# Layer 2's output columns parted as 256 and 320 instead of 288 and 288

## The chip, the cores and the metric

The kernel runs on one core of a Trainium2 chip. A core has a matrix engine (TensorE, "PE" in the profile, with its weight loads shown apart as "PEld"), a vector engine (VectorE, "DVE"), an activation engine (ScalarE, "ACT"), a general one (GpSimd, "POOL") and one that only issues transfers (SyncE, "SP"). The engines run at the same time and wait for each other by semaphores. [...] The metric is the device time of one execution in microseconds, the median of three runs for the kernel before.

## The reference

Two blocks work on 2048 tokens of 576 features, and their results are joined:

```
xn = layernorm(x)                                   # x: 2048 x 576
s  = S4D(xn)                                        # long convolution by FFT over the 2048 tokens
y  = layernorm(xn)
h  = gelu(y @ w1 + b1)                              # w1: 576 x 4608
g  = silu(h @ w2 + b2)                              # w2: 4608 x 576
out = x + s * g
```

The change is in the product `h @ w2`, called layer 2 below. Everything is float32 outside; the two large products are made from a rounded high part and a low rest, so that three fast products (high by high, high by low, low by high) give one accurate one.

## The kernel before

The MLP walks over 48 slots. The tokens come in two halves, each half in two blocks `tb` of 512 tokens; the 4608 hidden features come in 12 groups `g` of 3 x 128. A slot is one group for one block. It has 11 positions: three of layer 1 and eight of layer 2.

Layer 1 (`layer1`, line 529) makes 128 hidden features for 512 tokens with 14 matmuls, whose moving side is 512 columns wide. ScalarE then applies the gelu (line 547) and rounds the high part `hh` (line 550), and VectorE makes the low part `hl` (line 553).

Layer 2 (`layer2`, line 556) takes the 128 tokens `j` (0 to 3) of the block as stationary side and rows of w2 as moving side. w2's tiles are `w2h` (high) and `w2l` (low), each 128 partitions of 3 rows of 576 float32, 2304 bytes a row. [...] Each part of a block of 128 tokens takes three rows `i` by three products, nine matmuls (line 568). In a slot that makes 4 x 2 x 9 = 72, in the kernel 3456, half of them for each part. The result tile `q` has two banks: part 0 begins at the start of the first bank and part 1 at the start of the second. Tiles `mxa` and `mxb` take turns. When both parts are done, VectorE adds all 576 columns to the running sum `acc` in one instruction (line 576).

Only for the last 128 tokens of the last slot is each part added as soon as it is there (`halves`, line 1435); `finish` (line 633) then makes that part's silu (line 642), two VectorE steps (lines 647 and 657) and its output transfers (line 660). For the first half of the tokens, `gate_store` (line 584) makes a tanh over the two halves of 288 columns of the finished sum; the change leaves it alone.

The order of the work is written out ahead of time by a planner (`Order`, line 52). Steps have an engine, an estimated duration and a due time; the planner fills each engine's line between the matmuls, and the instructions of every engine are pinned in that order. Layer 2's estimated lengths stand in a list (line 1177), the additions' in line 1440. Beside the MLP run the pieces of the convolution (names `cv`, `kt`, `A2`, `f2t`, `g2t`), whose matmuls are put in between positions. Weights come in through the SP queue, which the change does not touch.

Of the kernel before, what the change touches and what calls it, by code (L numbers as in the profile page):

```python
# [17 lines left out]
L, D, N, F = 2048, 576, 128, 4608  # L18
# [14 lines left out]
G = 3  # L33
NG = F // (P * G)
KB = 4
TB = 512

def dve(n):  # L40
    return 0.075 + 0.00104 * n


def act(n):
    return 0.06 + 0.00098 * n
# [159 lines left out]
def step(eng, dur, fn, need=(), mark=None, cv=0, at=0.0, late=0.0, tbl=None, by=1e9):  # L205
    return dict(eng=eng, dur=dur, fn=fn, need=tuple(need), mark=mark, cv=cv, at=at, late=late, tbl=tbl, by=by)
# [3 lines left out]
def mixer_kernel(ctx, tc, u, log_a_real, a_imag, c_real, c_imag, log_dt, d_skip, w1, b1, w2, b2,  # L210
                 f1, f2, g2, g1, tvals, ident, out, parts=("mlp", "s4d")):
    nc = tc.nc
# [6 lines left out]
    def bank2(name):  # L219
        return ps.tile([P, 2, TB], F32, name=name, bufs=2 if name == "cv" else 1)  # L220

# [29 lines left out]
    bias2 = sb.tile([P, D], F32, name="bias2")  # L251
# [102 lines left out]
    acc = sb.tile([P, 8, D], F32, name="acc")  # L354
# [71 lines left out]

    XH = sb.tile([P, KB, 2, TB], F32R, name="XH")
    XL = sb.tile([P, KB, 2, TB], F32R, name="XL")
    XR = sb.tile([P, 2, TB], F32R, name="XR")
    dsk = sb.tile([P, D // 4], F32, name="dsk")  # L430
# [92 lines left out]
    HID, LAST, Q1, Q2 = {}, {}, {}, {}  # L523
    turn = [0]

    def mx(i):
        return "mxa" if (turn[0] + i) % 2 == 0 else "mxb"

    def layer1(g, tb, i):
# [11 lines left out]
        if i == 0:  # L541
            HID[tb] = (sb.tile([P, G, TB], F32R, name="hh"), sb.tile([P, G, TB], F32R, name="hl"))
        hh, hl = HID[tb]
        t = sb.tile([P, TB], F32, name="h32", bufs=2)

# [10 lines left out]
    def layer2(g, tb, j, terms, last):  # L556


        h, lo = W[2]
        hh, hl = HID[tb]  # L560
        c = slice(j * P, (j + 1) * P)
        if j not in Q2:
            Q2[j] = bank2(mx(j + 1))
        q = Q2[j]
        for i, dh in terms:
            d = slice(dh * 288, dh * 288 + 288)
            for k, (a, b) in enumerate(((hh, h), (hh, lo), (hl, h))):
                nc.tensor.matmul(q[:, dh, :288], a[:, i, c], b[:, i, d], start=i == 0 and k == 0,  # L568
                                 stop=i == G - 1 and k == 2)
        if last:  # L570
            Q2.pop(j)

        def add(dh, n):
            o = acc[:, tb * 4 + j].rearrange("p (h d) -> p h d", h=2)[:, dh:dh + n]
            b = bias2.rearrange("p (h d) -> p h d", h=2)[:, dh:dh + n]
            nc.vector.tensor_add(o, q[:, dh:dh + n, :288], b if g == 0 else o)  # L576
        return add

    def tanh_half(z):
# [19 lines left out]
    def rows_at(t, b, c0, c1):  # L599
        return [dram(t, (b + 16 * y) * D + c0, [[32 * D, 64], [1, c1 - c0]]) for y in range(2)]  # L600
# [32 lines left out]
    def finish(b, c0, c1, silu, end):  # L633

        c = slice(c0, c1)
        z = acc[:, b - 8, c]
        n = c1 - c0
        T = []

        def act_z():  # L640
            T.append(sb.tile([P, D], F32, name="row", bufs=NROW)[:, c])
            nc.scalar.activation(T[0], z, AF.Silu if silu else AF.Tanh, scale=1.0 if silu else 0.5)

        def mul():
            s = XS[b][1][:, c]
            if silu:
                nc.vector.scalar_tensor_tensor(s, s, 2.0, T[0], op0=OP.mult, op1=OP.mult)
            else:
                nc.vector.tensor_mul(s, s, z)

        def mul2():
            s = XS[b][1][:, c]
            nc.vector.scalar_tensor_tensor(s, T[0], 1.0, s, op0=OP.add, op1=OP.mult)

        def total():
            x, s = XS[b]
            nc.vector.tensor_add(x[:, c], x[:, c], s[:, c])
            for y, o in enumerate(rows_at(out, b, c.start, c.stop)):
                queue = nc.scalar if end and y else nc.sync
                queue.dma_start(o, x[64 * y:64 * y + 64, c])  # L660
        st = [step("ACT", act(n), act_z, tbl="silu" if silu else "gelu"), step("DVE", dve(n), mul)]
        if not silu:
            st.append(step("DVE", dve(n), mul2))
        return st + [step("DVE", dve(n), total)]
# [444 lines left out]
    NSLOT = 4 * NG  # L1109
# [142 lines left out]
    def wmark(n, which):  # L1252

        per = KB + 1 + G
        a = n * per + (0 if which == 1 else KB + 1)
        return [("w", k) for k in range(a, a + (KB + 1 if which == 1 else G))]
# [123 lines left out]
    def hidden_by(pos, i, o=0):  # L1380
        n = when(pos, o + (G if i < G - 1 else G + 2))
        low = n - dve(TB) - GAP
        high = low - act(TB) - GAP
        free = when(pos, o + (2, G, G + 1)[i])
        return min(high, free) - act(TB) - GAP, high, low
# [4 lines left out]
    def look_ahead(pos):  # L1390
        a, d = [], []
        for q in range(pos + 1, pos + 1 + NPOS):
            o, r = q // NPOS * NPOS, q % NPOS
            if r < G:
                b = hidden_by(pos, r, o)
                a.append(b[0])
                d.append(b[2])
            elif r - G in (2, 3, 5, 7):
                d.append(add_by(pos, (2, 3, 5, 7).index(r - G), o))
        od.next = dict(ACT=min(a), DVE=min(d))  # L1400

    for slot in range(NSLOT):
        turn[0] = slot
        g, tb = slot // 2 % NG, slot % 2
        n = slot // 2
        final = slot >= NSLOT - 2
        for pos in range(NPOS):
            if pos < G:
                need = wmark(n, 1) + [("x", tb)]
                if pos == 0:  # L1410
                    od.force(lambda: all(m in od.marks for m in need))
                cell = []
                od.unit(lambda: cell.append(layer1(g, tb, pos)), L1, need)
                look_ahead(pos)
                a, b, c = cell[0]
                by = hidden_by(pos, pos)
                od.urgent.append((od.t["PE"], [step("ACT", 0.62, a, tbl="gelu", by=by[0]),
                                               step("ACT", act(TB), b, by=by[1]),
                                               step("DVE", dve(TB), c, mark=("h", slot, pos), by=by[2])]))
                od.advance(od.t["PE"])  # L1420
                if pos == G - 1 and tb == 1 and slot + 1 < NSLOT:
                    weigh_in(1)
            else:
                j, terms, last, hid = l2_terms(pos - G)
                need = wmark(n, 2) + [("h", slot, i) for i in hid]
                if pos == G:

                    pe_turns()
                od.force(lambda: all(m in od.marks for m in need))
                if max(od.marks[m] for m in need) > od.t["PE"] + 0.3:  # L1430
                    pe_turns(any_time=True)
                cell = []
                od.unit(lambda: cell.append(layer2(g, tb, j, terms, last)), LEN[pos], need)
                look_ahead(pos)
                halves = slot == NSLOT - 1 and j == 3
                if last or halves:
                    add = cell[0]
                    dh, k = (terms[0][1], 1) if halves else (0, 2)
                    done = ("acc", slot, j, dh)
                    chain = [step("DVE", dve(288 * k), lambda: add(dh, k), mark=done, by=add_by(pos, j))]  # L1440
                    if final:
                        b = 8 + 4 * tb + j
                        x = el if slot < NSLOT - 1 else od.line()
                        st = finish(b, dh * 288, (dh + k) * 288, slot == NSLOT - 1, halves)
                        st[0]["need"] = (done, ("s8", b - 8))
                        x["steps"] += st
                    elif g == NG - 1:
                        for d in range(2):
                            one, two = gate_store(4 * tb + j, d)
                            by = od.t["PE"] + 5.0  # L1450
                            chain += [step("ACT", act(288), one, tbl="gelu", by=by), step("DVE", dve(288), two, by=by)]
                    od.urgent.append((od.t["PE"], chain))
                if pos == NPOS - 1 and tb == 1 and slot + 1 < NSLOT:
                    weigh_in(2)
            for f in LATER.get((slot, pos), ()):
                f()
            od.advance(od.t["PE"])
            pe_turns(all_lines=pos in (0, 1, 2, G + 1, G + 3, G + 5, NPOS - 1))
# [55 lines left out]
```

## Time and profile before

| What | Value |
|---|---|
| Median of 3 runs (lowest to highest) | 1124.04 us (1123.22 to 1124.32) |
| Profiled execution: its time, its span | 1126.06 us, 1124.3 us |
| PE busy, share of the span | 1106.2 us, 98% |
| Weight loads | 957.3 us, 85% |
| DVE busy | 880.0 us, 78% |
| ACT busy | 666.0 us, 59% |
| Mean granted clock of PE | 0.994 |
| Instructions | 26828 |

A matmul's duration in the profile reaches from its start to the end of its drain, and the next one starts before that; so the groups' mean durations are longer than the distance between two starts, and a long row of matmuls counts as one busy stretch. Weight loads run beside the matmuls. In the groups, `128*128 128x288` means a stationary side of 128 by 128 and a moving side of 128 partitions by 288 columns. Rows of the order of time give start and duration in microseconds; "x4" joins four of one kind. "Idle before" is the idle time of that engine ahead of an instruction, with what ended it.

### The profile page before, as it was taken

What the parts mean: (1) busy time and instruction counts of PE and PEld (TensorE: products, weight loads), DVE (VectorE), ACT (ScalarE), POOL (GpSimd) and SP (SyncE); (2) the same over time, 40 slices, a digit from 0 to 9 for tenths busy, and PEclk for the clock granted to TensorE, in tenths of its full rate; (3) what the DMA queues carried; (4) which work ended last, traced back from release to release, by engine and by line L of the source; (5) the groups of instructions that cost most, each with busy time, mean ns of one, the idle gap of its engine ahead of it and who ended that gap; (6) DMA issues with size and microseconds to landing.
All of it is one profiled execution on the core that took longest, in us unless ns stands there. A gap on an engine that the chain in (4) does not pass through costs nothing.

```text
span 1124.3 us, 26828 instructions
## 1 busy us (share of the span) xinstructions
PE 1106.2 (98%) x11355; PEld 957.3 (85%) x11355; DVE 880.0 (78%) x1475; ACT 666.0 (59%) x1011; POOL 183.1 (16%) x253
## 2 busy tenths in 40 slices
PE   9799999999999999999999999999999999999997
PEld 7698988988888788888888888887888978888896
DVE  6487688698879787999899889986898876555356
ACT  5297399976566475677956755654657433342233
POOL 5546401135110100001100010000000021112300
PEclk9899999999999999999999999999999999999999
DMA  7544645535353420443424242332315154534513
GB/s 217 208 152 122 219 159 183 162 113 126 106 167 92 107 82 13 142 108 104 155 56 137 34 123 56 111 85 63 91 50 126 33 169 136 163 103 142 151 60 85
DMA packets 111048, 132.39 MB, mean 118 GB/s; under 512 B 59660, under 2 KB 78192, under 8 KB 110352
## 3 DMA queue, kind: packets, MB, share of 16 engines
q1 hardware_dynamic: 96144, 79.88, 25.9%
q0 software_dynamic: 14304, 50.05, 14.1%
q8 instruction: 89, 1.46, 0.6%
q10 hardware_dynamic: 480, 0.74, 0.3%
q14 instruction: 31, 0.25, 0.1%
HBM read 101.87 MB, written 36.63 MB: 123 GB/s over the span
## 4 chain that ended last, share of the span: by engine, by line
PE 94%; issue 2%; DMA 1%; DVE 1%; ACT 1%; SPq 0%; POOL 0%; POOLq 0%; DVEq 0%; ACTq 0%
PE mxb L540 20%; PE mxb L568 20%; PE mxa L540 20%; PE mxa L568 20%; PE cv L885 3%; PE cv L1013 3%; PE cv L1055 2%; PE cv L986 2%; PE cv L955 2%; PE cv L1081 2%; DMA tv<-in_tvals_dram 1%; DMA kt<-in_A_A_imag_dram 1%; DMA raw<-in_B_w_dram 0%; PE cv L448 0%; DVE acc L576 0%
## 5 line engine op out<-in xcount | busy, mean ns | idle before, releaser
L553 DVE TENSOR_TENSOR hl<-h,hh 128x512 fp32r<-128x512 f32 x144 | 99.3, 692 | 129.4 <-ACT hh L550 128.9
L568 PE MATMUL mxb<-w2h,hh 128*128 128x288 f32 x576 | 172.2, 299 | 0.7 <-DVE acc L576 0.7
L568 PE MATMUL mxa<-w2h,hh 128*128 128x288 f32 x576 | 171.0, 297 | 0.0
L568 PE MATMUL mxb<-w2h,hl 128*128 128x288 f32 x576 | 170.3, 296 | 0.0
L568 PE MATMUL mxa<-w2h,hl 128*128 128x288 f32 x576 | 170.1, 295 | 0.0
L568 PE MATMUL mxb<-w2l,hh 128*128 128x288 f32 x576 | 169.4, 294 | 0.0
L568 PE MATMUL mxa<-w2l,hh 128*128 128x288 f32 x576 | 169.4, 294 | 0.0
L547 ACT ACTIVATE h<-mxb,b1t 128x512 f32<-128x512 f32 x72 | 49.6, 689 | 157.1 <-PE mxb L540 154.9
L568 PEld LDWEIGHTS mxb<-w2h,hh 128*128 128x128 f32 x576 | 108.1, 188 | 9.3 <-issue 4.1
L568 PEld LDWEIGHTS mxa<-w2h,hh 128*128 128x128 f32 x576 | 108.1, 188 | 6.2 <-issue 1.4
L568 PEld LDWEIGHTS mxa<-w2l,hh 128*128 128x128 f32 x576 | 108.2, 188 | 0.8
L568 PEld LDWEIGHTS mxb<-w2l,hh 128*128 128x128 f32 x576 | 108.2, 188 | 0.5
L568 PEld LDWEIGHTS mxb<-w2h,hl 128*128 128x128 f32 x576 | 108.1, 188 | 0.2 <-DVE hl L553 0.2
L568 PEld LDWEIGHTS mxa<-w2h,hl 128*128 128x128 f32 x576 | 108.1, 188 | 0.0
L786 POOL DMA_DIRECT2D par<-par_s x36 | 27.3, 760 | 479.6 <-DVE mg L829 475.5
L547 ACT ACTIVATE h<-mxa,b1t 128x512 f32<-128x512 f32 x72 | 49.6, 689 | 85.3 <-PE mxa L540 84.8
L576 DVE TENSOR_TENSOR acc<-mxb,acc 128x576 f32<-128x576 f32 (+1 forms) x89 | 66.3, 745 | 36.1 <-PE mxb L568 35.9
L550 ACT ACTIVATE hh<-h 128x512 fp32r<-128x512 f32 x144 | 90.6, 630 | 3.7
L576 DVE TENSOR_TENSOR acc<-mxa,acc 128x576 f32<-128x576 f32 x88 | 66.2, 752 | 28.3 <-PE mxa L568 27.6
L540 PE MATMUL mxa<-XH,w1h 128*128 128x512 f32 x288 | 81.7, 404 | 0.4 <-ACT XH L452 0.4
L540 PE MATMUL mxb<-XH,w1h 128*128 128x512 f32 x288 | 80.2, 401 | 0.1
L540 PE MATMUL mxb<-XL,w1h 128*128 128x512 f32 x288 | 78.1, 393 | 0.0
(215 smaller groups left out, 2395.2 us busy)
## 6 DMA issues: line engine op xcount, KB each, us to landing
raw<-in_B_w_dram SPq DMA_DIRECT2D x72, 288.0 KB, 3.2
raw<-in_B_w_dram SPq DMA_DIRECT2D x96, 192.0 KB, 3.6
par_s<-A POOLq DMA_DIRECT2D x4, 2160.0 KB, 8.1
par<-par_s POOLq DMA_DIRECT2D x36, 240.0 KB, 3.3
f2t<-f2q SPq DMA_DIRECT2D x24, 256.0 KB, 3.7
g2t<-g2p SPq DMA_DIRECT2D x24, 256.0 KB, 3.9
raw<-in_B_w_dram SPq DMA_DIRECT2D x48, 96.0 KB, 4.3
xc<-xn_s SPq DMA_DIRECT2D x48, 96.0 KB, 3.8
```

The costliest lines, as they stand in the source:

```text
L540: nc.tensor.matmul(q, a, b, start=j == 0, stop=j == len(ops) - 1)
L547: nc.scalar.activation(t, q, AF.Gelu_apprx_tanh, bias=b1t[:, g * G + i:g * G + i + 1], scale=1.0)
L550: LAST[0] = nc.scalar.activation(hh[:, i], t, AF.Copy)
L553: nc.vector.tensor_sub(hl[:, i], t, hh[:, i].bitcast(F32))
L568: nc.tensor.matmul(q[:, dh, :288], a[:, i, c], b[:, i, d], start=i == 0 and k == 0, stop=i == G - 1 and k == 2)
L576: nc.vector.tensor_add(o, q[:, dh:dh + n, :288], b if g == 0 else o)
L786: nc.gpsimd.dma_start(PAR[b].rearrange("p (g i) k -> p g (i k)", g=4), dram(par_s, (b // 3 * 48 + b % 3 * 4) * NPAR, [[D * NPAR, P], [12 * ...
L885: nc.tensor.matmul(q[32 * g:32 * g + 32, i // 2, i % 2 * 64:i % 2 * 64 + 64], U[:, ri, 4 * g + i, :], v[:, ri, 4 * g + i, :], start=ri == ...
L955: nc.tensor.matmul(Q[24 * v][:, e].rearrange("p d b -> p b d"), f1t[r, 0].rearrange("p f k -> p (f k)"), XC[i][r, :, 12 * e:12 * e + 12], ...
L986: nc.tensor.matmul(Q[g // 2 * 2][:, g % 2], f1t[r, (e + g) % 2].rearrange("p f k -> p (f k)"), KT[c, i][r, :, 32 * e:32 * e + 32], start=e ...
L1013: nc.tensor.matmul(Q[i][32 * q:32 * q + 32, f, 2 * ri:2 * ri + 2], m[r, 4 * i + q, 32 * ri:32 * ri + 32], A2[r, 4 * p + 2 * i + q // 2, :, ...
L1055: nc.tensor.matmul(QI[q // 2][64 * f:64 * f + 64, q % 2, i], MAT["g2t", p + i // 2][r, i % 2, f, ri], YS[p + i // 2][0][r, i % 2, ri, f], ...
```

## The change

Part 0 takes columns 0 to 255 and part 1 columns 256 to 575, so that the parts begin at bytes 0 and 1024 of a row of w2 (before: 0 and 1152). In PSUM the two parts now lie side by side across the border of the two banks: part 0 fills the last 256 places of the first bank, part 1 the first 320 of the second. The addition reads one run of 576 values instead of two runs of 288 with a gap. For the last 128 tokens the parts that are finished one by one have 256 and 320 columns. The planner's list of layer 2's lengths and the additions' estimate stay as they are.

```diff
 TB = 512
+DH = (0, 256, D)
...
         if j not in Q2:
-            Q2[j] = bank2(mx(j + 1))
+            Q2[j] = bank2(mx(j + 1)).rearrange("p h n -> p (h n)")
         q = Q2[j]
         for i, dh in terms:
-            d = slice(dh * 288, dh * 288 + 288)
+            d = slice(DH[dh], DH[dh + 1])
             for k, (a, b) in enumerate(((hh, h), (hh, lo), (hl, h))):
-                nc.tensor.matmul(q[:, dh, :288], a[:, i, c], b[:, i, d], start=i == 0 and k == 0,
-                                 stop=i == G - 1 and k == 2)
+                nc.tensor.matmul(q[:, TB - DH[1] + d.start:TB - DH[1] + d.stop], a[:, i, c], b[:, i, d],
+                                 start=i == 0 and k == 0, stop=i == G - 1 and k == 2)
...
         def add(dh, n):
-            o = acc[:, tb * 4 + j].rearrange("p (h d) -> p h d", h=2)[:, dh:dh + n]
-            b = bias2.rearrange("p (h d) -> p h d", h=2)[:, dh:dh + n]
-            nc.vector.tensor_add(o, q[:, dh:dh + n, :288], b if g == 0 else o)
+            d = slice(DH[dh], DH[dh + n])
+            o = acc[:, tb * 4 + j, d]
+            nc.vector.tensor_add(o, q[:, TB - DH[1] + d.start:TB - DH[1] + d.stop], bias2[:, d] if g == 0 else o)
         return add
...
-                        st = finish(b, dh * 288, (dh + k) * 288, slot == NSLOT - 1, halves)
+                        st = finish(b, DH[dh], DH[dh + k], slot == NSLOT - 1, halves)
```

## The prediction

> **What bounds the kernel now.** I read the page from the top (busy shares, then the chain that ended last), then the busy time by stretch, then the groups of matmuls by shape, and last the order of time in the last two slots. The page's head, its clock row and its chain:
>
> ```profile
> span 1124.3 us, 26828 instructions
> ...
> PE 1106.2 (98%) x11355; PEld 957.3 (85%) x11355; DVE 880.0 (78%) x1475; ACT 666.0 (59%) x1011; POOL 183.1 (16%) x253
> ...
> PEclk9899999999999999999999999999999999999999
> ...
> PE 94%; issue 2%; DMA 1%; DVE 1%; ACT 1%; SPq 0%; POOL 0%; POOLq 0%; DVEq 0%; ACTq 0%
> ```
>
> Two stretches of the table of busy time, one from the middle and the last (columns: stretch, its length, then busy time of PE, weight loads, DVE, ACT and POOL, granted clock, DMA share, GB/s):
>
> ```profile
> 300.00:400.00 100.00, 100.00 (x1216) 85.26 (x1215) 81.56 (x137) 60.24 (x83) 9.46 (x14) 1.00 0.43 118
> 1100.00:1124.00 24.00, 16.32 (x101) 14.74 (x99) 14.34 (x23) 8.77 (x13) 0.00 (x0) 0.92 0.37 87
> ```
>
> TensorE makes 94% of the chain. In the middle it is busy for 100.00 of 100.00 us at clock 1.00, while DVE is busy for 81.56. So the time is the number of matmuls times the distance between the starts of two of them, and then a tail. The change touches the matmuls of line 568, so their form and the forms next to it matter:
>
> ```profile
> L568 PE MATMUL mxb<-w2h,hh 128*128 128x288 f32 x576 | 172.2, 299 | 0.7 <-DVE acc L576 0.7
> L540 PE MATMUL mxb<-XL,w1h 128*128 128x512 f32 x288 | 78.1, 393 | 0.0
> L1013 PE MATMUL cv<-A,f2t 64*32 64x192 f32 x1536 | 38.6, 333 | 0.0
> L986 PE MATMUL cv<-kt,f1t 32*128 32x384 f32 x192 | 18.9, 507 | 0.0
> L568 PEld LDWEIGHTS mxb<-w2h,hh 128*128 128x128 f32 x576 | 108.1, 188 | 9.3 <-issue 4.1 <-DVE acc L576 1.5 <-ACT hh L550 0.9
> L1081 PEld LDWEIGHTS cv<-A,g1t 128*64 128x64 f32 x96 | 6.4, 134 | 7.9 <-issue 7.5
> L885 PEld LDWEIGHTS cv<-v,U 128*32 128x32 f32 x2304 | 33.8, 110 | 9.4 <-issue 9.1 <-DVE hl L553 0.4
> ```
>
> Line 568 stands in six such groups of 576, so 3456 matmuls: 1728 for the left half of the columns, 1728 for the right. The 299 ns of one is from its start to the end of its drain; the next starts before that, so the cost is the distance of starts. That is read in order of time. Here are the first matmuls of four runs of nine in the last slot but one (left, right, left, right half; rows between left out), then the first of layer 1, and another 14 matmuls later:
>
> ```profile
> 1092.06 0.30 PE L568 MATMUL mxb<-w2h,hh 128*128 128x288 f32 x1
> ...
> 1093.25 0.29 PE L568 MATMUL mxb<-w2h,hh 128*128 128x288 f32 x1
> ...
> 1094.45 0.29 PE L568 MATMUL mxa<-w2h,hh 128*128 128x288 f32 x1
> ...
> 1095.63 0.29 PE L568 MATMUL mxa<-w2h,hh 128*128 128x288 f32 x1
> ...
> 1096.83 1.08 PE L540 MATMUL mxb<-XH,w1h 128*128 128x512 f32 x4
> ...
> 1100.02 1.07 PE L540 MATMUL mxa<-XH,w1h 128*128 128x512 f32 x4
> ```
>
> The 36 matmuls of 288 columns take 1096.83 - 1092.06 = 4.77 us, 132.5 ns each. The 14 of 512 columns take 3.19 us, 227.9 ns each. That is (227.9 - 132.5) / 224 = 0.426 ns for a column, and 132.5 - 288 x 0.426 = 9.8 ns for a matmul whatever its width.
>
> **The change part by part.**
>
> *Columns.* Each left matmul loses 32 columns and each right one gains 32: 132.5 - 13.6 = 118.9 ns and 132.5 + 13.6 = 146.1 ns. The pair stays at 265.0 ns, the count stays at 3456, and so do the weight loads. Sum over 1728 pairs: 0.
>
> *The start of the right part.* It moves from byte 1152 of a row of w2's tiles to byte 1024. The four runs above show what a start at 1152 costs now: left (start 0) 1.19 and 1.18 us, right 1.20 and 1.20 us, so 2.37 / 18 = 131.7 ns against 2.40 / 18 = 133.3 ns. Rows are cut to 10 ns, so the gap of 1.6 ns has about a nanosecond of doubt. Taken over the start times of all the matmuls of line 568 whose successor is of that line (distances under 160 ns), the means are 131.6 ns left and 133.0 ns right, a gap of 1.4 ns. The first and the last of them:
>
> ```profile
> L568 PE MATMUL mxb<-w2h,hh x576: 288/294/402, 24.1 to 1116.5; 128*128 128x288 f32 x192
> ...
> L568 PE MATMUL mxb<-w2h,hl x576: 289/295/398, 24.4 to 1116.7; 128*128 128x288 f32 x192
> ```
>
> If that gap is the price of the start, 1.4 x 1728 = 2.4 us are to be had. Upwards, the new widths could carry the gap with them and double it, +2.4 us. Downwards, if both parts fell by one and a half times the gap, 2.1 x 3456 = 7.3 us. I take 0, because right and left differ in their PSUM bank and in their place in the order too, so that the rows don't tie the gap to the start. [...]
>
> *The weight load under a narrower matmul.* Each matmul has its own load of 128 columns, issued when the matmul before it starts. In the last slot TensorE once waited for a result to be read, and there the load shows uncovered:
>
> ```profile
> 1114.56 0.29 PE L568 MATMUL mxb<-w2h,hl 128*128 128x288 f32 x1
> 1115.05 0.45 DVE L576 TENSOR_TENSOR acc<-mxb,acc 128x288 f32<-128x288 f32 x1
> ...
> 1115.56 0.19 PEld L568 LDWEIGHTS mxb<-w2h,hh 128*128 128x128 f32 x1 [0.93 <-DVE acc L576]
> 1115.56 0.40 PE L568 MATMUL mxb<-w2h,hh 128*128 128x288 f32 x1 [0.70 <-DVE acc L576]
> 1115.66 0.19 PEld L568 LDWEIGHTS mxb<-w2l,hh 128*128 128x128 f32 x1
> 1115.79 0.29 PE L568 MATMUL mxb<-w2l,hh 128*128 128x288 f32 x1
> ```
>
> The next start is 0.23 us later instead of 0.13, so the load itself takes 0.10 us. The groups of loads say the same: 110, 134 and 188 ns for 32, 64 and 128 columns, (188 - 110) / 96 = 0.81 ns for a column, 104 ns for 128, and some 84 ns of latency that overlaps. Transposes, whose moving side is 128 wide and which each have a load of 128 columns, start every 0.11 us ((0.60 - 0.27) / 3):
>
> ```profile
> 10.96 0.60 PE L448 MATMUL cv<-idp,row 128*128 128x128 f32 x4
> 11.29 0.14 PEld L448 LDWEIGHTS mxb<-idp,row 128*128 128x128 f32 x1
> 11.39 0.27 PE L448 MATMUL mxb<-idp,row 128*128 128x128 f32 x1
> ```
>
> So 104 to 110 ns of load have to fit under 118.9 ns: covered, with 9 to 15 ns to spare instead of 23 to 29. From below it costs 0. From above, the 256 columns could cost no less than 288 do now: 13.6 x 1728 = 23.5 us. I take 0, by the load that stands uncovered in this very group.
>
> *DVE's addition (line 576).* Its PSUM input becomes one run of 576 instead of two of 288, the same number of elements; its price now:
>
> ```profile
> L576 DVE TENSOR_TENSOR acc<-mxa,acc 128x576 f32<-128x576 f32 x88 | 66.2, 752 | 28.3 <-PE mxa L568 27.6
> L576 DVE TENSOR_TENSOR acc<-mxb,acc 128x288 f32<-128x288 f32 x2 | 0.9, 454 | 0.9 <-PE mxb L568 0.9
> ```
>
> It is taken as 752 ns again. TensorE covers it: the group of line 568 above waits for DVE 0.7 us in the whole run. If each of the 192 additions were 10% longer and uncovered, 14 us; but the 28.3 us of idling ahead of 88 of them is 0.32 us each, cover for the 0.08.
>
> *Planner.* The costs that the order of work is planned with stay as they were (288 a half) save in the last block's closing steps, so instructions, queues and DMAs keep their order and count.
>
> *Tail.* Only the last block works half by half. Its closing rows now:
>
> ```profile
> 1116.73 0.29 PE L568 MATMUL mxb<-w2h,hl 128*128 128x288 f32 x1
> 1117.05 0.46 DVE L576 TENSOR_TENSOR acc<-mxb,acc 128x288 f32<-128x288 f32 x1 [0.89 <-PE mxb L568]
> 1117.43 0.75 DVE L647 SCALAR_TENSOR_TENSOR A<-A,row 128x576 f32<-128x576 f32 x1
> 1118.21 0.76 DVE L657 TENSOR_TENSOR v<-v,A 128x576 f32<-128x576 f32 x1
> 1118.89 0.45 DVE L647 SCALAR_TENSOR_TENSOR A<-A,row 128x288 f32<-128x288 f32 x1
> 1119.37 0.46 DVE L657 TENSOR_TENSOR v<-v,A 128x288 f32<-128x288 f32 x1
> 1119.75 0.45 DVE L647 SCALAR_TENSOR_TENSOR A<-A,row 128x288 f32<-128x288 f32 x1
> 1120.23 0.46 DVE L657 TENSOR_TENSOR v<-v,A 128x288 f32<-128x288 f32 x1
> ```
>
> A column costs DVE (752 - 454) / 288 = 1.03 ns, so 32 columns are 0.03 us. The left addition (1115.05) starts when DVE is free, not when TensorE is, so its earlier input gives nothing; it is 0.03 shorter. The nine right matmuls then take 9 x 13.6 = 0.12 us longer and the right addition 0.03 longer; the two steps left and two right that follow cancel. Sum: +0.12 us. The wait of 0.7 us could go, since the halves lie in separate banks; it is there now although they do already, so I leave it: at best -0.9 us. The last output rows are 1280 bytes instead of 1152, at most 0.1 us more.
>
> **Sum.** 0 + 0 + 0 + 0.12 = +0.1 us. The profiled execution took 1126.06 us, its span 1124.3 and 1.8 around it; it would go to 1126.2. The median of the runs is 1124.04 (1123.22 to 1124.32), 2.0 lower, so the forecast is 1124.2 us. A difference under 0.2% (2.2 us) counts as none: it is about what a measurement of this kernel can tell from no change.
>
> **The rivals.**
>
> *Slower: the load no longer fits.* Place: the 1728 left matmuls. If a matmul can begin only when both the stream before it and its load are done, and the hand-over of 9.8 ns comes after the later of the two, the distance is 104 to 110 plus 9.8 and 3 for the load's later start, 117 to 123 ns against 118.9. At 123 it is 4.1 x 1728 = +7.1 us, 1131 us; it decides (over 2.2 us) from 120.2 ns on. For it: the loads' busy share of 85%, and no row with such a narrow matmul of this type and load. Against it: the transposes' 0.11. [...]
>
> *Faster: the start was the gap.* The right matmuls then run with the left ones' fixed part: -2.4 us, with the tail 1121.8 us; more, if the left gains too, down to 1117. For it: the gap is there in every pair of runs. Against it: bank and order differ as well.
>
> *Far slower: the fast rate ends at 256 columns.* Lines 1013 and 986 run the full type, (507 - 333) / 192 = 0.91 ns a column, against (393 - 299) / 224 = 0.42 for 568 and 540. At that rate 256 columns cost 0.49 x 256 = 125 ns more, 1728 times: +216 us, 1340 us. No row is narrower than 288 in the fast type, so the trace can't exclude it.
>
> **How the numbers follow.** No change 0.34; the load 0.30; the start 0.28; the rate 0.05; a slower tail or DVE in the way 0.03. So faster 0.28, same 0.34, slower 0.38. The likeliest alone: 1122 to 1126.4. Since the other two hold more than half, the range takes them in: down to 1117 (both parts gaining) and up to 1136 (the load at 125.7 ns). That leaves out the rate and the ends of the others, under 0.2.
>
> **What would show it.** The distance of starts in line 568: 118.9 and 146.1 ns, sum 265.0. If the load is in the way, the left ones stand at 120 to 126 and the right ones at 146; if the start matters, the right ones stand below 145; if the rate ends, the left ones stand near 240. DVE's 752 ns and the one wait of 0.7 us stay. Wrong would be a pair off 265.0 by more than 1.3 ns, or new idle time ahead of line 568.

## The result and the profile after

The changed kernel took 1126.65 us (median of 9 runs, 1125.95 to 1128.37); the kernel before took 1124.40 us beside it (9 runs, 1122.40 to 1125.18). The ratio is 1.0024, with a 95% interval of 1.0014 to 1.0035: slower by a quarter of a per cent. The forecast was 1124.2 us in a range of 1117 to 1136, with no change (within 0.2%) as the likeliest case. The time lies in the range, 0.25 us above the band of the likeliest case (1122 to 1126.4); the interval of 0.14 to 0.35% doesn't shut out a difference under 0.2%.

The page of the changed kernel, the lines that answer to those shown of before (line numbers are higher by one):

```profile
span 1124.7 us, 26828 instructions
...
PE 1107.8 (98%) x11355; PEld 958.8 (85%) x11355; DVE 880.1 (78%) x1475; ACT 666.0 (59%) x1011; POOL 183.1 (16%) x253
...
PE 96%; DVE 1%; DMA 1%; ACT 1%; SPq 0%; issue 0%; ACTq 0%
```

The instructions are the same in number on every engine, and TensorE still makes the chain. So the cause has to be sought in the distances between matmuls. The same four runs of nine as in the prediction (left, right, left, right part, then layer 1), in the order of time of TensorE:

```profile
1092.30 0.28 PE L569 MATMUL mxb<-w2h,hh 128*128 128x256 f32 x1
...
1093.38 0.31 PE L569 MATMUL mxb<-w2h,hh 128*128 128x320 f32 x1
...
1094.70 0.28 PE L569 MATMUL mxa<-w2h,hh 128*128 128x256 f32 x1
...
1095.78 0.31 PE L569 MATMUL mxa<-w2h,hh 128*128 128x320 f32 x1
...
1097.10 0.39 PE L541 MATMUL mxb<-XH,w1h 128*128 128x512 f32 x1
```

The 36 matmuls take 1097.10 - 1092.30 = 4.80 us; before they took 4.77. Nine of 256 columns take 1.08 us (120 ns each), nine of 320 take 1.32 (147 ns each). That is small, and so each distance below is a mean over the whole trace: all starts of layer 2's matmuls whose successor is of layer 2 too and follows within 175 ns, some 1,670 for each part (fewer in one kernel, noted there). Before: 131.6 ns left, 133.0 right, 264.7 a pair. After: 119.4 left, 147.0 right, 266.4 a pair. There are 1728 pairs: 1.7 x 1728 = 2.9 us, against 2.25 us between the two medians.

The two profiled executions differ by less, 1124.3 and 1124.7 us of span. The chains show why. The row of the same 18 matmuls, early in the run, before and after:

```profile
61.04 2.38 PE mxa L568 x18
```

```profile
58.37 2.40 PE mxa L569 x18
```

The profiled run of before had lost 2.7 us by then, at its start: its transposes waited 7.1 us for DVE's `XL`, those of the changed kernel 4.5 us. From that row to the start of the last matmul it took 1116.73 - 61.04 = 1055.69 us, the changed kernel 1117.13 - 58.37 = 1058.76: 3.1 us more in the steady part. The tail, from the start of the left addition to the end of the last step on DVE:

```profile
1115.38 0.42 DVE L577 TENSOR_TENSOR acc<-mxb,acc 128x256 f32<-128x256 f32 x1
...
1115.85 0.41 PE L569 MATMUL mxb<-w2h,hh 128*128 128x320 f32 x1 [0.78 <-DVE acc L577]
...
1117.13 0.31 PE L569 MATMUL mxb<-w2h,hl 128*128 128x320 f32 x1
1117.48 0.49 DVE L577 TENSOR_TENSOR acc<-mxb,acc 128x320 f32<-128x320 f32 x1 [1.01 <-PE mxb L569]
...
1120.65 0.49 DVE L658 TENSOR_TENSOR v<-v,A 128x320 f32<-128x320 f32 x1
```

It is 1120.65 + 0.49 - 1115.38 = 5.76 us; before it was 1120.23 + 0.46 - 1115.05 = 5.64. So the tail gives +0.12 us, and the rest, some 3 us of it in the distances of layer 2, is what had to be explained.

### The profile page after: what moved, and what is told of

Same layout as the page of the kernel before. It is cut to its first block, busy times and chain, and to the rows that moved or that the text cites. A ratio compares the mean times of both kernels' runs of the same rounds, so it can differ in the third digit from the quotient of the medians.

```text
span 1124.7 us, 26828 instructions
## 1 busy us (share of the span) xinstructions
PE 1107.8 (98%) x11355; PEld 958.8 (85%) x11355; DVE 880.1 (78%) x1475; ACT 666.0 (59%) x1011; POOL 183.1 (16%) x253
## 4 chain that ended last, share of the span: by engine, by line
PE 96%; DVE 1%; DMA 1%; ACT 1%; SPq 0%; issue 0%; ACTq 0%
PE mxa L541 21%; PE mxb L541 21%; PE mxb L569 20%; PE mxa L569 20%; PE cv L886 3%; PE cv L1014 3%; PE cv L1056 2%; PE cv L987 2%; PE cv L956 2%; PE cv L1082 2%; DMA tv<-in_tvals_dram 0%; DMA acc<-in_A_u_dram 0%; DMA raw<-in_B_w_dram 0%; DVE acc L577 0%; PE cv L449 0%
## 5 line engine op out<-in xcount | busy, mean ns | idle before, releaser
L554 DVE TENSOR_TENSOR hl<-h,hh 128x512 fp32r<-128x512 f32 x144 | 99.2, 692 | 129.8 <-ACT hh L551 129.5
L569 PE MATMUL mxb<-w2h,hh 128*128 128x256 f32 (+1 forms) x576 | 173.4, 301 | 0.8 <-DVE acc L577 0.8
L569 PE MATMUL mxa<-w2h,hh 128*128 128x256 f32 (+1 forms) x576 | 172.2, 299 | 0.0
L569 PE MATMUL mxb<-w2h,hl 128*128 128x256 f32 (+1 forms) x576 | 170.5, 296 | 0.0
L569 PE MATMUL mxa<-w2l,hh 128*128 128x256 f32 (+1 forms) x576 | 170.4, 296 | 0.0
L569 PE MATMUL mxa<-w2h,hl 128*128 128x256 f32 (+1 forms) x576 | 170.4, 296 | 0.0
L569 PE MATMUL mxb<-w2l,hh 128*128 128x256 f32 (+1 forms) x576 | 170.4, 296 | 0.0
```

Of the source, the lines that this page charges most:

```text
L554: nc.vector.tensor_sub(hl[:, i], t, hh[:, i].bitcast(F32))
L569: nc.tensor.matmul(q[:, TB - DH[1] + d.start:TB - DH[1] + d.stop], a[:, i, c], b[:, i, d], start=i == 0 and k == 0, stop=i == G - 1 and k ...
```

## The experiments

The change does three things at once in layer 2: other widths, another start of the right part in w2's rows, and another place in PSUM with a flat addition. Here a place in PSUM is one in the tile that the kernel's `bank2` makes, 2 x 512 values a partition. Four theories could each give 1.7 ns a pair: width (the distance is set by the number of columns), start (by where the moving row begins), PSUM place or addition, and the weight load (no longer covered by 256 columns). All distances of this study, worked out as above, with the time that 1728 pairs make of the difference to before, and the measured ratio to the kernel before:

| Kernel | left, ns | right, ns | pair, ns | 1728 x difference, us | ratio (95% interval) |
|---|---|---|---|---|---|
| before (288, 288) | 131.6 | 133.0 | 264.7 | | |
| after (256, 320) | 119.4 | 147.0 | 266.4 | +2.9 | 1.0024 (1.0014 to 1.0035) |
| 288, 288, new place in PSUM | 131.6 | 133.1 | 264.7 | 0.0 | 1.0007 (0.9998 to 1.0016) |
| 256, 320, old place in PSUM | 119.4 | 147.0 | 266.3 | +2.9 | one run, 1127.72 us |
| 288, 288, starts turned | 132.8 | 133.1 | 265.8 | +2.0 | 1.0024 (1.0012 to 1.0036) |
| 272, 304 | 125.4 | 138.2 | 263.6 | -1.9 | 0.9989 (0.9980 to 0.9998) |
| 272, 304, again | 125.4 | 138.1 | 263.5 | -2.0 | 0.9984 (0.9974 to 0.9994) |
| 288, 288, w2 moved by 128 bytes | 133.1 | 131.9 | 265.0 | +0.6 | 1.0009 (1.0000 to 1.0019) |
| 256, 320, w2 moved by 128 bytes | 118.7 | 147.0 | 265.7 | +1.7 | 1.0018 (1.0008 to 1.0027) |
| 320, 256 | 146.8 | 119.6 | 266.4 | +2.9 | one run, 1127.97 us |
| 192, 384 | 109.0 | 173.1 | 282.1 | +30 | one run, 1158.77 us |
| 288, 288, w2 and hidden tiles moved | 131.7 | 133.1 | 264.7 | +0.1 | one run, 1124.80 us |
| 280, 296 | 128.0 | 137.0 | 265.1 | +0.7 | 1.0005 (0.9996 to 1.0014) |
| 304, 272 | 138.0 | 124.9 | 262.8 | -3.2 | one run, 1120.32 us |

The distances explain the times: where an interval was measured, 1728 times the difference, over 1124, lies in it each time. For 192 and 384 columns the +30 us is short of the 35.1 us between its one time and the median beside it, since the limit of 175 ns leaves out slow distances there; all distances from a matmul of layer 2 to the next matmul, whatever that is, add up to 36.1 us more than before.

**Old widths in the new place.** The changed kernel with one number put back:

```diff
-DH = (0, 256, D)
+DH = (0, 288, D)
```

> Parts of 288 and 288 again, but in the new place in PSUM (side by side across the border of the banks) and with the addition as one run of 576. Changed kernel: left 119.4, right 147.0 ns between starts, 266.4 a pair; before: 131.6 and 133.0, 264.6. Theory width (the distance depends on the number of columns alone): 131.6 and 133.0 again, time as before, ratio 1.000. Theory PSUM place or addition: the pair stays at 266.4, ratio 1.0024. Theory start of the right part (1152 instead of 1024 bytes costs or saves): as width, since the start is 1152 again; the run with turned starts tells these two apart.

Two pairs of nine runs, from the first left matmul to the second and to layer 1:

```profile
1090.20 0.30 PE L569 MATMUL mxb<-w2h,hh 128*128 128x288 f32 x1
...
1092.58 0.29 PE L569 MATMUL mxa<-w2h,hh 128*128 128x288 f32 x1
...
1094.96 0.39 PE L541 MATMUL mxb<-XH,w1h 128*128 128x512 f32 x1
```

2.38 us for 18, twice, as before (2.39 and 2.38). Left and right are those of before to 0.1 ns, and so is the order of long and short distances within a slot. The place in PSUM and the flat addition make no difference to the pair here, 264.7 ns in both. This theory falls.

**New widths in the old place.** Parts of 256 and 320, each at the start of its bank, and the addition in two instructions:

```diff
-                nc.tensor.matmul(q[:, TB - DH[1] + d.start:TB - DH[1] + d.stop], a[:, i, c], b[:, i, d],
+                nc.tensor.matmul(q[:, dh, :d.stop - d.start], a[:, i, c], b[:, i, d],
...
+            for e in range(dh, dh + n):
+                d = slice(DH[e], DH[e + 1])
+                o = acc[:, tb * 4 + j, d]
+                nc.vector.tensor_add(o, q[:, e, :d.stop - d.start], bias2[:, d] if g == 0 else o)
```

> Parts of 256 and 320, each at the start of its bank of PSUM as before; the addition in two instructions (256 and 320). Theory width or start: 119.4 and 147.0, 266.4 a pair, as in the changed kernel. Theory PSUM place: 264.6 a pair. DVE has 176 more instructions, some 0.1 us each, beside TensorE.

119.4 and 147.0: the changed kernel's pair with the old place. The other half of the same finding: where the columns are cut is the cause.

**Starts turned.** The kernel before, with w2's tiles laid out part by part instead of row by row:

```diff
-                W[2] = (sb.tile([P, G, D], F32R, name="w2h"), sb.tile([P, G, D], F32R, name="w2l"))
+                W[2] = (sb.tile([P, 2, G, 288], F32R, name="w2h"), sb.tile([P, 2, G, 288], F32R, name="w2l"))
...
-            h, lo, m = h[:, i], lo[:, i], P
+            h, lo, m = h[:, :, i], lo[:, :, i], P
...
-                nc.tensor.matmul(q[:, dh, :288], a[:, i, c], b[:, i, d], start=i == 0 and k == 0,
+                nc.tensor.matmul(q[:, dh, :288], a[:, i, c], b[:, dh, i], start=i == 0 and k == 0,
```

> The kernel before, but w2's tiles hold the three left parts and then the three right parts, 1152 bytes each, so that left rows begin at 0, 4.5 and 9 times 256 bytes and right rows at 13.5, 18 and 22.5 times. Theory start: the matmuls of left row 1 and right rows 0 and 2 run at one distance, those of left rows 0 and 2 and right row 1 at another, about 1.4 ns apart. Theory width: the distances stay with the part (131.6 left, 133.0 right), or all change alike; time as before, ratio 1.000 (0.999 to 1.001).

```profile
1092.74 0.30 PE L568 MATMUL mxb<-w2h,hh 128*128 128x288 f32 x1
...
1093.94 0.29 PE L568 MATMUL mxb<-w2h,hh 128*128 128x288 f32 x1
...
1095.14 0.30 PE L568 MATMUL mxa<-w2h,hh 128*128 128x288 f32 x1
...
1096.34 0.29 PE L568 MATMUL mxa<-w2h,hh 128*128 128x288 f32 x1
...
1097.54 0.40 PE L541 MATMUL mxb<-XH,w1h 128*128 128x512 f32 x1
```

Now all four runs take 1.20 us, where left ones took 1.19 and 1.18. By row: left 131.7, 134.0 and 132.5 ns; right 133.4, 132.8 and 133.1. A block is the author's unit here: 256 bytes or 64 columns, counted from the beginning of w2's tile. The three that begin at whole blocks (left 0 and 2, right 1) have a mean of 132.4, the other three of 133.5. The start counts, as that theory has it, but the pair did not stay at 264.7: it grew by 1.1 ns, and the time with it. So at one width the distance went from 131.7 to 134.0 ns by row: width alone doesn't set it either.

**w2's tiles moved.** An unused tile of 128 bytes ahead of them, in the kernel before and in the changed one:

```diff
+            if k == KB + 1:
+                nc.gpsimd.memset(sb.tile([P, 32], F32, name="pad"), 0.0)
             if i == 0:
```

> The kernel before, with an unused tile of 128 bytes put ahead of w2's two tiles, so that left rows now begin half a block of 256 bytes later and right rows where left rows stood against the block; one small memset on GpSimd is added. Theory start (a moving row that begins in the middle of a block of 256 bytes costs about 1.4 ns more than one that begins at its border): left and right change places, left 133.0, right 131.6 ns, pair 264.6, ratio 1.000. Theory order or bank of PSUM: left stays 131.6, right 133.0, ratio 1.000. Theory that the whole address counts in some other way: other distances than these, pair between 263 and 267.

The four runs of 288 and 288, w2's tiles moved:

```profile
1089.28 0.29 PE L570 MATMUL mxb<-w2h,hh 128*128 128x288 f32 x1
...
1090.48 0.30 PE L570 MATMUL mxb<-w2h,hh 128*128 128x288 f32 x1
...
1091.67 0.29 PE L570 MATMUL mxa<-w2h,hh 128*128 128x288 f32 x1
...
1092.86 0.29 PE L570 MATMUL mxa<-w2h,hh 128*128 128x288 f32 x1
...
1094.05 0.40 PE L542 MATMUL mxb<-XH,w1h 128*128 128x512 f32 x1
```

The first left run now takes 1.20 us and the right ones 1.19. Over the trace left is 133.1 and right 131.9: they have changed places. So the gap of 1.4 ns in the kernel before went with the start, not with the bank or the order, which stayed.

> The changed kernel (256 and 320) with the same unused tile of 128 bytes, so that both parts begin half a block of 256 bytes later. Theory width (256 and 320 cost columns / 2.4 and 13.3 ns wherever they begin): 119.4 and 147.0, 266.4 a pair, ratio 1.0024. Theory start (common starts set the distance): both parts change, and if half a block costs 1.4 ns each, 269.2 a pair, ratio 1.005; if the common border is what costs, 264.6 or less, ratio 1.000.

With 256 and 320 the pair is 265.7, between what the theories gave: the move of w2's tiles gives 118.7 instead of 119.4 left and spares nothing right. In these runs a start at a whole block is thus the dear one for 256 columns (119.4 against 118.7 ns), the cheap one for 288 (131.6 against 133.1), and no matter for 320 (147.0 in both).

**Both operands moved.** The same unused tile ahead of `hh` and `hl`, which moves these and w2's tiles alike:

```diff
+            if g == tb == turn[0] == 0:
+                nc.gpsimd.memset(sb.tile([P, 32], F32, name="pad"), 0.0)
             HID[tb] = (sb.tile([P, G, TB], F32R, name="hh"), sb.tile([P, G, TB], F32R, name="hl"))
```

> The kernel before with the unused tile of 128 bytes put ahead of hh and hl, so that the stationary tiles move by half a block together with w2's tiles. Theory that the start of the moving row alone counts: as with w2's tiles moved alone, left 133.1 and right 131.9 ns. Theory that the place of the moving row against the stationary one counts (loads and moving reads meeting): as before, left 131.6 and right 133.0.

```profile
1090.71 0.30 PE L570 MATMUL mxb<-w2h,hh 128*128 128x288 f32 x1
...
1091.89 0.29 PE L570 MATMUL mxb<-w2h,hh 128*128 128x288 f32 x1
...
1093.09 0.29 PE L570 MATMUL mxa<-w2h,hh 128*128 128x288 f32 x1
...
1094.27 0.29 PE L570 MATMUL mxa<-w2h,hh 128*128 128x288 f32 x1
...
1095.47 0.39 PE L540 MATMUL mxb<-XH,w1h 128*128 128x512 f32 x1
```

1.18, 1.20, 1.18, 1.20: left and right as before, 131.7 and 133.1. Even by row it is the kernel before: the right rows 0, 1 and 2 took 132.3, 134.2 and 132.6 ns there, and the same again here. Moving w2 alone turned the parts round; moving w2 and the stationary tiles together did not. w2's tiles lie at the same place in both of these runs, and only `hh` and `hl` differ. So between these two runs (left 133.1 and 131.7 ns) the distance followed where the moving row lies against the stationary operand, not its address. The half block is not the whole of it, though: those three right rows all begin in the middle of a block and are up to 1.9 ns apart, and the left matmuls of the kernel before, which all begin at whole blocks, took 129.8 ns for `w2h` with `hh`, 131.5 for `w2l` with `hh` and 133.5 for `w2h` with `hl`. The stationary tiles are read by the weight loads, which run while the moving rows stream: in the trace of the kernel before, a load of layer 2 starts 3 ns (median) after the start of a matmul and takes 188 ns. The 1.4 ns in 133 between left and right follow the two operands' places; whether the loads cause it, no run here shows.

**Turned parts, and the floor.**

```diff
-DH = (0, 256, D)
+DH = (0, 320, D)
```

> Parts turned: 320 columns left, 256 right (start at byte 1280, five times 256). Theory that widths and starts in whole blocks set the distance: left 147, right 120 ns, pair 266.4, as in the changed kernel. Theory that the order (narrow before wide) matters: a pair other than 266.4 by more than 1 ns.

146.8 and 119.6, the same pair of 266.4: narrow before wide or wide before narrow made no difference.

```diff
-DH = (0, 256, D)
+DH = (0, 192, D)
```

> Parts of 192 and 384 columns (start at byte 768, three times 256). Theory that the weight load is covered at 256 and has a floor of 104 to 110 ns: left at 104 to 112 ns instead of 93.3 (192 / 2.4 and 13.3), right at 173.3, pair 278 to 285. Theory that the hand-over of some 10 ns comes after the load: left at 114 to 120. Theory that the load never shows: 93.3 and 173.3, 266.6. Theory that the fast rate ends at or below 256 columns: left above 170.

One run of nine narrow matmuls, with the first two of the next run:

```profile
1123.38 0.25 PE L569 MATMUL mxb<-w2h,hh 128*128 128x192 f32 x1
1123.47 0.28 PE L569 MATMUL mxb<-w2l,hh 128*128 128x192 f32 x1
1123.59 0.27 PE L569 MATMUL mxb<-w2h,hl 128*128 128x192 f32 x1
1123.70 0.28 PE L569 MATMUL mxb<-w2h,hh 128*128 128x192 f32 x1
1123.81 0.27 PE L569 MATMUL mxb<-w2l,hh 128*128 128x192 f32 x1
1123.92 0.27 PE L569 MATMUL mxb<-w2h,hl 128*128 128x192 f32 x1
1124.03 0.27 PE L569 MATMUL mxb<-w2h,hh 128*128 128x192 f32 x1
1124.14 0.28 PE L569 MATMUL mxb<-w2l,hh 128*128 128x192 f32 x1
1124.26 0.27 PE L569 MATMUL mxb<-w2h,hl 128*128 128x192 f32 x1
1124.37 0.36 PE L569 MATMUL mxb<-w2h,hh 128*128 128x384 f32 x1
1124.57 0.33 PE L569 MATMUL mxb<-w2l,hh 128*128 128x384 f32 x1
```

Here a floor shows. From the second to the ninth the distances are 0.11 or 0.12 us, mean over the trace 111.7 ns inside a run, where the line of the expectations gives 93. The first after a wide run stands at 0.09, and the first wide one after a narrow run pays 0.20. The author puts all three down to the load, which the rows of before gave 104 to 110 ns: done in time after a wide run, not done otherwise. No run shows that apart from the distances. (The mean of the 384 columns in the table leaves these first ones out, with all others of 175 ns and more: 1,172 of 1,661 distances are left.) So the floor stands at 111 to 112 ns, below the 114 to 120 expected of a load with a hand-over of 10 ns behind it, and the 119.4 ns of 256 columns lie above it. If the floor is the load's, the load is not what made the change slower. Nor does the fast rate end at 256 columns, nor at 192: 111.7 ns, where the 0.91 ns a column of lines 1013 and 986 would make 175.

**Parts off the blocks.**

> The changed kernel with parts of 272 and 304. Theory width with a step at 64 columns (256 and 320 pay a full fixed part of 13.3 ns over columns / 2.4, 288 one of 12.3): 272 and 304 lie off the multiples of 64 as 288 does, fixed parts of 12.3, 125.6 and 139.0, 264.6 a pair, ratio 1.000. Theory start: 1088 bytes is no multiple of 256 either, so as before, 264.6. Theory that only a pair of equal widths is spared: 126.7 and 140.0, 266.7, ratio 1.0024.

> 272 and 304 once more, for a narrower interval: pair 263.6 ns, 1.1 less than before, 1.1 x 1728 = 1.9 us, ratio 0.9983 by the distances alone; 0.9980 to 0.9998 by the first measurement.

```diff
-DH = (0, 256, D)
+DH = (0, 272, D)
```

125.4 and 138.2, 263.6 a pair: 1.1 ns below the kernel before, and below all three theories of the first run (264.6, 264.6 and 266.7). It was faster in two measurements (0.9989 and 0.9984, both intervals below 1).

> Parts of 280 and 296 columns (right start at byte 1120). Columns / 2.4 and 13.3 ns would be 130.0 and 136.7, 266.7 a pair, ratio 1.0024. Theory that parts which are no whole number of blocks of 64 columns, or begin inside a block, are spared some of the 13.3: 263.5 to 265, ratio 0.998 to 1.001. Theory that 288 and 272 are special: 266.4 a pair.

```diff
-DH = (0, 256, D)
+DH = (0, 280, D)
```

128.0 and 137.0, 265.1 a pair: a little above the 263.5 to 265 expected of parts off the blocks, and well below the 266.4 expected if only 288 and 272 were special. The left part is spared 2.0 ns of its 130.0; the right one, at 137.0, nothing.

> Parts of 304 and 272 (right start at byte 1216). If only start and width of each matmul count, its pair need not be that of 272 and 304 (263.6), since both starts differ: 263 to 265. If the pair is 263.6 within 0.3 ns, the sum of widths off the block counts, not the starts.

```diff
-DH = (0, 256, D)
+DH = (0, 304, D)
```

```profile
1086.47 0.30 PE L569 MATMUL mxb<-w2h,hh 128*128 128x304 f32 x1
...
1087.71 0.29 PE L569 MATMUL mxb<-w2h,hh 128*128 128x272 f32 x1
...
1088.85 0.30 PE L569 MATMUL mxa<-w2h,hh 128*128 128x304 f32 x1
...
1090.09 0.29 PE L569 MATMUL mxa<-w2h,hh 128*128 128x272 f32 x1
...
1091.20 0.39 PE L541 MATMUL mxb<-XH,w1h 128*128 128x512 f32 x1
```

36 matmuls in 4.73 us, against 4.77 before and 4.80 after the change. The pair is 262.8, 0.2 ns below the lowest that was expected (263 to 265) and 0.8 below that of 272 and 304, so the starts counted here and not only the sum of widths. Its one time, 1120.32 us against a median of 1123.63 for the kernel before beside it, is 3.3 us lower, as 1.9 x 1728 = 3.2 us would have it; it is one run, so no interval stands behind it. By the runs that have one, 272 and 304 beats the kernel before by 0.16% (0.06 to 0.26%), and so the changed one too.

**What the distances say together.** The widths tried that are whole multiples of 64 columns (256 bytes), begun at whole blocks, lie near one line: 119.4 for 256, 147.0 for 320, 173.1 for 384, 227 for layer 1's 512 columns (the median of its distances). 0.417 ns a column and 13.3 ns for each matmul, the line of the expectations ("columns / 2.4"), gives them to within 0.7 ns: (227 - 147.0) / 192 is 0.417, and above that rate the four stand at 12.7, 13.7, 13.1 and 13.7 ns. Least squares through the four give 0.419 and 12.3, so the fixed part is known to about a nanosecond only, but the costs of the widths between 256 and 320 differ by no more than 0.3 ns between the two lines. On the first 288 would cost 133.3, 272 126.7, 280 130.0, 296 136.7 and 304 140.0. Measured were 131.6 (start at a block) and 133.0 (start in the middle) for 288, 125.4 and 124.9 for 272, 128.0 for 280, 137.0 for 296, 138.2 and 138.0 for 304. All but one of these widths off the blocks are spared something, up to 2 ns, though 288 in the middle of a block hardly more than the 0.3 ns of doubt. The old cut was spared 1.7 and 0.3 ns; the new one came to 266.4 ns a pair, and the line gives 266.7.

## Why the prediction came out as it did

*Bound.* Right. TensorE makes the chain before and after, and 1728 pairs times the difference of a pair gives the time within the interval wherever one was measured.

*Columns: "The pair stays at 265.0 ns".* This step failed. The pair was 266.4 ns, so by the prediction's own sign (a pair off 265.0 by more than 1.3 ns) its account was wrong, though its range held. The prediction drew a line through two widths, 288 and 512, and read off 0.426 ns a column and 9.8 ns fixed, which gave 118.9 and 146.1 ns for 256 and 320 columns. Measured were 119.4 and 147.0. Half their sum is 133.2, and 288 itself had stood at 132.35 (half of its pair of 264.7): it lies 0.85 ns below the straight line through its two neighbours. So the 32 columns saved less on the left than they cost on the right, by 1.7 ns a pair, which is the whole 2.9 us. The base was 0.3 ns high as well, since 265.0 came from rows cut at 10 ns; the prediction's own means over the trace, 131.6 and 133.0, make 264.6. With two points a line always fits, and one of them was the odd one. That columns times a rate and a fixed part describe the widths from 256 to 512 to 2 ns was right, but what the change did lay inside these 2 ns.

*Start: taken as 0, with -2.4 us as a rival.* The gap between left and right was indeed the start's: it changed sides when w2's tiles were moved. But the rival's time did not come: of the three widths tried at both places, a start at a whole block was the cheap one for 288 alone. At 256 columns moving the start off the block spared 0.7 ns, and at 320 it changed nothing. The rival took one part's saving over to another width; that was its error. Its other end, "the new widths could carry the gap with them and double it, +2.4 us", was near in size, for another reason.

*Load: taken as covered.* Right by the 192 columns: a floor of 111 to 112 ns (104 to 110 had been estimated for the load) under 119.4 ns. The rival that forecast 1131 us had the side right and the reason wrong; a hand-over of 9.8 ns behind the load did not show at 192 columns, 111.7 ns against 114 to 120.

*Rate: 0.05.* Did not happen; 256 columns stand at 119.4 ns.

*Addition and planner.* Right: 752 and 753 ns for the addition in the groups of the changed kernel, and 26828 instructions in both.

```profile
L577 DVE TENSOR_TENSOR acc<-mxa,acc 128x576 f32<-128x576 f32 x88 | 66.2, 752 | 29.6 <-PE mxa L569 29.0
L577 DVE TENSOR_TENSOR acc<-mxb,acc 128x576 f32<-128x576 f32 x87 | 65.5, 753 | 35.5 <-PE mxb L569 35.0
```

*Tail: +0.12 us, with the one wait left in place.* Right: 5.76 against 5.64 us, and the wait is there, 0.78 us.

*Sum.* +0.1 us forecast, +2.25 us between the medians measured: +0.12 from the tail, about +2.9 from the pairs by the trace. The likeliest case missed by the columns' step. The range held because it took in the rivals, and that was luck as far as the mechanism goes: the time came out on the slower side by none of the reasons that the prediction had for it.

## What to carry to other kernels

When a kernel is bound by thousands of like matmuls, a nanosecond in the distance of their starts is a measurable time (here 1.7 ns a pair made 2.9 us), so read that distance over the whole trace and by kind (part, row, product) before moving a cut; a mean duration or two rows at 10 ns don't show it. Don't take a per-column price from two widths if one of them may be special; a third width on the chip costs one run. A cut at round byte addresses is no gain by itself: here it put both parts on the full line, and parts of 272 and 304 columns, neither a whole number of blocks, were faster than both kernels (0.9989 and 0.9984 of the kernel before, the changed one 1.0024).

## What was not expected of the hardware

In these runs the distance between two matmuls went with where the moving row lies against the stationary operand: 131.6 or 133.0 ns at 288 columns, turned round by moving one operand by 128 bytes and restored by moving both. Widths off whole blocks of 64 columns came out up to 2 ns below the line of the whole ones (128.0 against 130.0 for 280). Why whole blocks pay the full line (119.4 to 227 ns for 256 to 512 columns) is open, and so is which relation of the two operands is best. No run gave two parts of 288 columns that both begin at whole blocks in every row, so what that would save is open too. The starts of 304 and 272 gave the lowest pair here, 262.8 ns.
